# A spectral-mixer kernel: smaller first loads, a part-major tile for the first filter piece, and a fixed order of the front on each engine

## The chip, the cores and the metric

The kernel runs on one core of one Trainium2 chip. The metric is the device time of one execution in microseconds (us); lower is better. The runs of one kernel mostly lie within one per cent of each other, and all but one count as undisturbed ("fast", granted TensorE clock 0.996 to 1.0). The one slow run belongs to one experiment (`e12_all`) and is left out of its ratio. Each profile shows one execution, so small differences between two profiles are those of single runs.

Short names used throughout: PE is the matmul engine (TensorE), DVE is VectorE, ACT is ScalarE, POOL is GpSimd, SP is SyncE. Times "at 21.48" are us from the start of the profiled span.

## The reference, cut to what matters

```
def reference(A_x, A_w_r, A_w_i, B_x, B_w1, B_b1, B_w2, B_b2):
    # A: layernorm, 2-D real FFT, product with a complex filter, inverse FFT
    X = rfft2(layernorm(x));  X = X * (w_r + 1j * w_i);  y = irfft2(X)
    h = x + y
    # B: layernorm, token-mixing MLP over the 2048 positions
    h2 = h + mlp(layernorm(h))          # 2048 -> 1376 -> 2048, gelu between
    return h2
```

x is 1 x 2048 x 512 in bf16, and the filter is 2048 x 257, real and imaginary. The kernel does the FFTs as matmuls. Its stages, and the names that the code and the profile give them:

1. **Front.** Load X in pieces and the DFT factors FP in four pieces. Layernorm statistics of 16 slices (`bn`/`ag` on DVE, or two ACT passes `s1`/`s2`), their reciprocal root `rs` on ACT, then the factors scaled by it (`fs`: FS<-FP,rs). Matmuls `f1`, evicted to Y.
2. **V stage.** Eight units u = 0 to 7. For each: matmuls `f2`, evicted to CS; matmuls `x`; the product with the filter on DVE (`v`: V<-ps,W); matmuls `g1`, evicted to PQ.
3. `g2`, `g3` and the additions on DVE (TT, H, HH).
4. The MLP on PE alone, the output additions (OUT) and the stores.

## The kernel before: the parts that matter

The order of the instructions on each engine is not written by hand. Each operation is declared with its inputs, its outputs, an assumed duration and a priority. A list scheduler in the kernel then picks, step by step, the ready operation with the earliest start, and takes the higher priority on a tie:

```
    def schedule(self):
        ...
        while len(order) < len(ops):
            best = None
            for o in ready:
                ...                       # PSUM bank free? limit of open units reached?
                st = max(eng_free[o.stream], o.dep_ready, avail, o.not_before)
                key = (st, -o.prio, o.idx)
                if best is None or key < best[0]:
                    best = (key, o, st, bank)
            ...
            eng_free[e] = st + o.occ
            if o.is_dma:
                x0 = max(st + (3200.0 if st < 4000.0 else 1700.0), dma_free)
                dma_free = x0 + o.bytes / o.rate
```

The scheduled order is then final: the engine runs it as listed.

The loads of the front and of the first filter piece (12 issues: for real and imaginary part w, two components, three kinds of rows):

```
    for q, (a, b) in enumerate(((0, 2), (2, 4), (4, 6), (6, 8), (8, 12))):
        ldx(a, b, 90 - q)                 # on SyncE; ldx(0, 2) is 256 KB
    ...
    ldf(0, 90, "act")                     # FP pieces of 256 KB; these two on ScalarE
    ...
    ldf(1, 87, "act", 1800.0)
    ...
        for w, dram in ((0, A_w_r), (1, A_w_i)):
            for comp in range(2):
                d = W[comp::4, g0:g0 + ng, w, :]
                lst.append(dma(f"ld_wp{ch}_{w}{comp}", d, ...))
                d = W[2 + comp::4, h0:h0 + nh, w, :]
                lst.append(dma(f"ld_wm{ch}_{w}{comp}", d, ...))
                if g0 == 0:
                    d = W[2 + comp::4, 0, w, :]
                    lst.append(dma(f"ld_wz{ch}_{w}{comp}", d, ...))
```

The V stage of one unit. The `x` matmuls need both CS tiles of the unit, and the multiply needs all eight `x` matmuls:

```
    def stage_x(u):
        unit = PsumUnit("x", 2)
        grp = [cs_ops[2 * u + 1]]
        for i in range(2):
            G = 2 * u + i
            ...
                    mm(f"x_{G}_{c}{r}", ..., CS[rows, G, :, c, :], unit, ..., 13, 256, half=True, after=grp)
        ...
        nh = 2 if u in V_SPLIT else 1     # V_SPLIT = (0, 7): two halves by group
        for h in range(nh):
            ...
            K.op(f"v_{u}_{h}", "dve", tt, ins=[wt], outs=[vout], occ=50.0 + 2130.0 / nh, ...)
```

## Time and profile before

| | before |
|---|---|
| device time, median of 3 (range) | 134.13 us (133.91 to 134.17) |
| profiled execution, and its span | 133.9 us, 132.4 us |
| first X pieces landed | 4.87 us |
| first `f2` matmul | 18.62 us |
| V multiplies on DVE | 21.48 to 39.36 us, without a gap |
| first TT addition | 42.63 us |
| last OUT addition ends, to the end of the device time | 3.92 us |

Almost half of the span (68 to 129 us) is bound by PE alone, at full clock, and apart from the loads the change works on the first 68 us only. The busy shares show this. Each digit is the busy share of one fortieth of the span (3.3 us) in tenths:

```profile
PE   6989989999977979999999999999999999999990
DVE  0499867999981999999960000000242332423322
ACT  4579976978966999986689322222000000000000
PEclk9999999999999999999999999999999999999999
```

The chain of work that ended last, in order of time (start, duration, what ran), has these long pieces in the first 43 us:

```profile
0.72 4.15 DMA X<-in_A_x_dram
4.89 1.34 ACT JK L549 x4
6.51 0.95 POOL FS L633
...
17.10 1.47 ACT Y L549 x3
18.62 2.77 PE ps L531 x25
21.48 1.04 DVE V L739
22.62 15.62 DVE V L739 x8
38.38 0.62 PE ps L531 x8
...
42.63 0.42 DVE TT L790
```

Read it as a relay: the first load until 4.87, then statistics and POOL and ACT in turn until 18.6, a short stretch of PE, and then DVE's multiplies end to end. DVE's own list of that stretch gives start, duration, operation and count, and in brackets the idle time just before and what ended it:

```profile
19.86 0.69 DVE L712 CAST CS<-ps 128x512 bf16<-128x512 f32 x1 [0.92 <-PE ps L531]
21.48 17.88 DVE L739 TENSOR_TENSOR V<-ps,W 128x1024 bf16<-128x1024 f32 x10 [0.94 <-PE ps L531]
42.63 0.42 DVE L790 TENSOR_TENSOR TT<-ps,X 128x256 f32<-128x256 f32 x1 [3.27 <-PE ps L531]
```

Ten multiplies, 17.88 us, one line: no idle time between them. In the front, DVE's list shows what waits for the loads:

```profile
4.89 0.70 DVE L653 BATCH_NORM_STATS2 st<-X 128x6 f32<-128x512 bf16 x1 [3.78 <-DMA X<-in_A_x_dram]
...
6.13 1.35 DVE L653 BATCH_NORM_STATS2 st<-X 128x6 f32<-128x512 bf16 x2 [0.32 <-DMA X<-in_A_x_dram]
```

And the windows view (length, then busy time and count of PE, weight loads, DVE, ACT, POOL, then granted clock, DMA share and GB/s) shows ACT full between 10 us and the first `f2`, busy for 8.53 of 8.60 us:

```profile
10.00:18.60 8.60, 8.05 (x62) 5.49 (x62) 7.61 (x24) 8.53 (x23) 7.02 (x13) 1.00 0.89 260
```

### The profile page before, as it was taken

What the parts mean: (1) busy time and instruction counts of PE and PEld (TensorE: products, weight loads), DVE (VectorE), ACT (ScalarE), POOL (GpSimd) and SP (SyncE); (2) the same over time, 40 slices, a digit from 0 to 9 for tenths busy, and PEclk for the clock granted to TensorE, in tenths of its full rate; (3) what the DMA queues carried; (4) which work ended last, traced back from release to release, by engine and by line L of the source; (5) the groups of instructions that cost most, each with busy time, mean ns of one, the idle gap of its engine ahead of it and who ended that gap; (6) DMA issues with size and microseconds to landing.
All of it is one profiled execution on the core that took longest, in us unless ns stands there. A gap on an engine that the chain in (4) does not pass through costs nothing.

```text
span 132.4 us, 2013 instructions
## 1 busy us (share of the span) xinstructions
PE 123.7 (93%) x776; PEld 74.5 (56%) x786; DVE 69.3 (52%) x127; ACT 63.3 (48%) x146; POOL 12.4 (9%) x33
## 2 busy tenths in 40 slices
PE   6989989999977979999999999999999999999990
PEld 2436656788666736544434444456666666666660
DVE  0499867999981999999960000000242332423322
ACT  4579976978966999986689322222000000000000
POOL 0199920000300000000000000000000000000000
PEclk9999999999999999999999999999999999999999
DMA  2999699999999999992000000000111112111121
GB/s 80 375 396 364 153 244 273 286 322 283 419 426 417 410 408 411 417 295 74 0 0 0 0 0 0 5 0 0 40 40 70 49 40 82 42 57 62 40 79 40
DMA packets 16648, 22.16 MB, mean 167 GB/s; under 512 B 2720, under 2 KB 12960, under 8 KB 16128
## 3 DMA queue, kind: packets, MB, share of 16 engines
q1 hardware_dynamic: 16352, 21.52, 47.5%
q10 hardware_dynamic: 288, 0.52, 1.1%
q8 instruction: 6, 0.10, 0.3%
q14 instruction: 2, 0.02, 0.0%
HBM read 19.95 MB, written 2.10 MB: 167 GB/s over the span
## 4 chain that ended last, share of the span: by engine, by line
PE 51%; DVE 32%; ACT 9%; DMA 3%; POOL 2%; issue 1%; DVEq 0%; ACTq 0%
PE ps L531 50%; DVE V L739 13%; DVE H L799 7%; ACT Y L549 5%; DVE TT L790 4%; DVE TT L792 4%; DVE HH L804 4%; DMA X<-in_A_x_dram 3%; POOL FS L633 1%; ACT rs L549 1%; ACT FS L549 1%; ACT JK L549 1%; DVE OUT L829 1%; ACT PQ L549 0%; PE ps L621 0%
## 5 line engine op out<-in xcount | busy, mean ns | idle before, releaser
L531 PE MATMUL ps<-HH,W 128*128 128x512 bf16 (+1 forms) x173 | 40.3, 379 | 1.3 <-DVE HH L804 0.9
L531 PE MATMUL ps<-GT,W 128*128 128x512 bf16 (+1 forms) x172 | 37.9, 379 | 0.2
L829 DVE SCALAR_TENSOR_TENSOR OUT<-ps,B2f,H 128x512 bf16<-128x512 f32 x16 | 12.0, 750 | 48.7 <-PE ps L531 48.7
L531 PEld LDWEIGHTS ps<-GT,W 128*128 128x128 bf16 (+1 forms) x176 | 25.3, 144 | 12.8
L531 PEld LDWEIGHTS ps<-HH,W 128*128 128x128 bf16 (+1 forms) x176 | 17.2, 100 | 21.2 <-DVE HH L804 1.9
L739 DVE TENSOR_TENSOR V<-ps,W 128x2048 bf16<-128x2048 f32 (+1 forms) x10 | 17.9, 1856 | 0.9 <-PE ps L531 0.9
L549 ACT ACTIVATE GT<-ps,B1f 128x512 bf16<-128x512 f32 (+1 forms) x11 | 7.1, 689 | 14.6 <-PE ps L531 14.6
L549 ACT ACTIVATE JK<-H,nm 128x512 bf16<-128x512 bf16 x16 | 11.6, 722 | 3.0 <-DVE H L799 2.9
L653 DVE BATCH_NORM_STATS2 st<-X 128x6 f32<-128x512 bf16 x14 | 9.2, 669 | 4.1 <-DMA X<-in_A_x_dram 4.1
L621 PE MATMUL ps<-ZT 128*128 128x512 bf16 x32 | 9.6, 434 | 1.6 <-DVE ZT L617 1.2
L799 DVE TENSOR_TENSOR H<-ps,TT 128x512 bf16<-128x512 f32 x16 | 10.9, 682 | 0.0
L549 ACT ACTIVATE PQ<-ps 128x512 bf16<-128x512 f32 x16 | 8.9, 602 | 3.5 <-PE ps L531 3.3
L531 PE MATMUL ps<-EM,PQ 128*128 128x256 bf16 x64 | 9.0, 273 | 0.8 <-ACT PQ L549 0.7
L531 PE MATMUL ps<-EM,V 128*128 128x128 bf16 x128 | 9.2, 219 | 0.5 <-DVE V L739 0.5
L549 ACT ACTIVATE EO<-ps 128x512 bf16<-128x512 f32 x16 | 9.2, 596 | 0.9 <-PE ps L531 0.9
L549 ACT ACTIVATE CS<-ps 128x512 bf16<-128x512 f32 x15 | 8.3, 607 | 2.1 <-PE ps L531 2.1
L531 PE MATMUL ps<-EM,Y 128*128 128x256 bf16 x64 | 8.7, 273 | 0.4 <-ACT Y L549 0.4
L531 PE MATMUL ps<-FS,X 128*128 128x256 bf16 x64 | 8.4, 274 | 0.5 <-POOL FS L633 0.4
L531 PEld LDWEIGHTS ps<-EM,V 128*128 128x128 bf16 x128 | 7.5, 98 | 2.3 <-issue 1.4
L633 POOL TENSOR_SCALAR FS<-FP,rs 128x256 bf16<-128x256 bf16 x9 | 8.6, 965 | 0.6 <-ACT rs L549 0.5
L790 DVE TENSOR_TENSOR TT<-ps,X 128x256 f32<-128x256 f32 x16 | 6.7, 417 | 3.3 <-PE ps L531 3.3
L531 PEld LDWEIGHTS ps<-EM,PQ 128*128 128x128 bf16 x64 | 6.2, 98 | 2.9 <-ACT PQ L549 0.9
(36 smaller groups left out, 79.1 us busy)
## 6 DMA issues: line engine op xcount, KB each, us to landing
W<-in_B_w_dram SPq DMA_DIRECT2D x4, 1376.0 KB, 11.7
W<-in_B_w_dram SPq DMA_DIRECT2D x10, 512.0 KB, 18.3
out_dram<-OUT SPq DMA_DIRECT2D x16, 128.0 KB, 1.7
W<-in_A_w_r_dram SPq DMA_DIRECT2D x4, 257.0 KB, 4.5
W<-in_A_w_i_dram SPq DMA_DIRECT2D x4, 257.0 KB, 5.0
X<-in_A_x_dram SPq DMA_DIRECT2D x4, 256.0 KB, 5.0
X<-in_A_x_dram SPq DMA_DIRECT2D x2, 512.0 KB, 6.6
W<-in_A_w_r_dram SPq DMA_DIRECT2D x4, 192.8 KB, 3.3
```

What stands on the lines that cost most here:

```text
L531: return K.op(name, "pe", lambda eng, bank: eng.matmul(outf(bank), lhsT, rhs, start=start, stop=stop), ins=ins or [lhsT, rhs], occ=occ, la ...
L549: return eng.activation(dst, s, func, **kw)
L621: return K.op(name, "pe", lambda eng, bank: eng.matmul(ps[:, bank, :], ZT[:, 0:NP], ZT[:, :], start=True, stop=True), ins=[ZT[:, :]], occ= ...
L633: dve(f"fs{i}", lambda eng, bank: eng.tensor_scalar(FS[:, i, :, :], FP[:, i, :, :], rs, None, op0=ALU.mult), [FP[:, i, :, :], rs], [FS[:, ...
L653: dve(f"st_{i}", lambda eng, bank, i=i, x=x: eng.bn_stats(ST[:, i, 0:6], x), [x], [ST[:, i, 0:6]], 512, prio=25)
L739: return eng.tensor_tensor(vout, s, win, ALU.mult)
L790: dve(f"tl_{s2}", lambda eng, bank, tt=tt, xl=xl: eng.tensor_tensor(tt[:, 0, :], ps[:, bank, 256:512], xl, ALU.add), [xl], [tt[:, 0, :]], ...
L792: dve(f"th_{s2}", lambda eng, bank, tt=tt, xh=xh: eng.tensor_tensor(tt[:, 1, :], xh, ps[:, bank, 256:512], ALU.subtract), [xh], [tt[:, 1, ...
L799: return eng.tensor_tensor(hs.rearrange("p (h d) -> p h d", h=2), e, tt[:, :, :], ALU.add)
L804: dve(f"hh_{s2}", lambda eng, bank, s2=s2, hs=hs: eng.tensor_scalar(HH[:, s2, :], hs, NM[:, s2:s2 + 1], R2[:, s2:s2 + 1], op0=ALU.add, op1 ...
L829: dve(f"fin{s2}", lambda eng, bank, dst=dst, bia=bia, hs=hs: eng.scalar_tensor_tensor(dst, ps[:, bank, :], bia, hs, op0=ALU.add, op1=ALU.add),
```

## The change

Its intent: start the statistics earlier (a first X piece of 128 KB, with the two FP pieces held behind a short zero fill), balance the front over the engines in an order that is listed in the kernel and so fixed, and load the first filter piece with 8 issues instead of 12 into a tile W0 of its own, in which real and imaginary part are the outer index. The two first multiplies then split by part instead of by group. The core of the diff:

```diff
 def _row(sign, comp, k2, s):
-    return 4 * (k2 * 2 + s) + 2 * sign + comp
+    return 4 * (k2 * 2 + s) + 2 * comp + sign
...
+                if o.name in pos and done[pos[o.name][0]] != pos[o.name][1]:
+                    continue             # fixed order for the named operations of an engine
...
-                x0 = max(st + (3200.0 if st < 4000.0 else 1700.0), dma_free)
-                dma_free = x0 + o.bytes / o.rate
+                x0 = max(st + 1750.0, dma_free) + o.stall
+                dma_free = x0 + o.bytes / (min(o.rate, 340.0) if x0 < 7000.0 else o.rate)
...
-STAT_ACT = (1, 3)
...
+STAT_ACT = (3, 6)
+FS_ENG = {4: 'act', 7: 'act', 9: 'act', 12: 'dve', 14: 'dve'}
...
+FRONT = {
+    "dve": """bn_0 bn_1 ag_1 ag_0 bn_2 bn_4 bn_5 ag_2 bn_7 ...""",
+    "act": """rs_1 rs_0 s1_3 s2_3 rs_3 s1_6 rs_2 s2_6 rs_4 ...""",
+    "pool": """fs_1 fs_0 bv_3 fs_3 fs_2 bv_6 fs_5 fs_6 ...""",
+    "pe": """f1_1 f1_0 f1_3 f1_4 f1_5 f1_2 f1_6 ...""",
+}
-V_SPLIT = (0, 7)
+V_SPLIT = (7,)
...
-    for q, (a, b) in enumerate(((0, 2), (2, 4), (4, 6), (6, 8), (8, 12))):
-        ldx(a, b, 90 - q)
+    for q, (a, b) in enumerate(((0, 1), (1, 2), (2, 4), (4, 6), (6, 8), (8, 12))):
+        ldx(a, b, 99 - q)
...
-    ldf(0, 90, "act")
-    ldf(1, 87, "act", 1800.0)
+    ldf(0, 92, "act", after=[zt])
+    ldf(1, 91, "act", after=[zt])
-    dma("ld_E", ...)
-    dma("ld_MR", ...)
+    dma("ld_EMR", ...)
...
+            if g0 == 0:
+                d = W0[0:NP:2, w, :, :].rearrange("p g l -> p (g l)")
+                lst.append(dma(f"ld_wp{ch}_{w}", d, ...))
+                d = W0[1:NP:2, w, 0, :]
+                lst.append(dma(f"ld_wz{ch}_{w}", d, ...))
...
+        if u == 0:
+            for w in range(2):
+                wt = W0[:, w, :, :]
...
+                K.op(f"v_0_{w}", "dve", tw, ins=[wt], outs=[vout], occ=1115.0, lat=1235.0, ...)
+            return
```

Also: the Y evictions become partly 1024 columns wide, two small POOL operations per ACT-computed statistic become one ahead of its `rs`, and the limit of open `f1` units rises from 6 to 7. For the V stage of units 1 to 7 the diff changes only the row order of the filter and of the matrices that go with it (`_row`), not the operations.

## The prediction

> **What bounds the kernel now.** The page gives 132.4 us of span, PE busy 93%, DVE 52%. The chain that ended last splits it into stretches with different limits:
> - 0.7 to 4.9 us: the first X piece is loading (DMA, 4.15 us).
> - 4.9 to 18.6 us: statistics, scaled DFT factors FS, Y evictions. First ACT and GpSimd in turn (FS on POOL, 0.95 us each), from about 10 us ACT: the windows show it busy 8.53 of 8.60 us.
> - 18.6 to 21.5: F2 and X matmuls (2.8 us), then VectorE: ten V multiplies without a gap (21.5 to 39.4), and from 42.6 to 68 the TT/H/HH operations (DVE busy 25.33 of 25.4 us).
> - 68 to 129: PE alone, clock 1.0.
>
> Everything after 18.6 us is saturated on DVE or PE, and the change leaves its work as it was. So only the front can gain.
>
> **What the change does.**
> 1. The first load becomes 128 KB alone on SyncE; ScalarE issues its two FP pieces only after the 0.27 us zero fill. Before, X0 (256 KB) and FP0 (256 KB) start together at 0.72 us and share the engines: DMA moves nothing until about 2.3 us and runs at 390 GB/s from 3.0, and X0 lands at 4.87. My estimate: x0 at about 3.4, x1 about 4.0, FP0 about 4.6 us. The Trainium skill (DMA: Bandwidth & Descriptors, "Issuing engines are not separate DMA queues") says that issuing from several engines saves only issue time, so total landing (x4 on) should not move.
> 2. First FS on POOL starts at about 5.4 instead of 6.51 us. But 20 warm-up matmuls hold PE until about 7.1, and the FS chain on POOL becomes longer: 11 scalings (0.93 us pitch) and two small ones against 9.
> 3. ScalarE in the front: same four statistics passes, 12 rs against 13, same three FS, evictions of 6144 instead of 6656 columns in 10 instead of 13 instructions. At 0.49 us per 512 columns, with about 0.06 us fixed per instruction, that is about 0.6 us less. VectorE takes 512 columns more, two FS fewer.
> 4. First filter piece: 8 issues instead of 12. At 0.65 us each, later loads are issued about 2.6 us earlier. Off the critical path: DVE never waited for W.
> 5. The first two V multiplies split by real/imaginary part, not by group: same 2 x 1.2 us.
>
> Adding the measured durations along each engine's new order (the same sum for the old order gives F2 at 18.5 against 18.62 measured), the three engines become nearly level: last POOL FS ends near 16.7, last Y evictions near 17.7 us, F2 starts at about 17.8, the first V multiply at 20.5 instead of 21.48. With landings 0.5 us later it is 18.2 and 20.9; earlier ones give nothing more.
>
> **Prediction.** A gain of about 0.9 us (0.3 to 1.6), which the saturated rest passes on unchanged: 133.2 us, 132.5 to 133.9. Chances: faster by over 2% 0.04, within 2% 0.94, slower 0.02.
>
> **What would show it.** x0 landing before 3.8 us; first bn_stats at 3.4 instead of 4.89; first POOL FS about 5.4; F2 near 17.8; V's length unchanged at 17.9 us, only shifted; 42.6-to-68 and the PE stretch shifted, not shortened.
>
> **What would make it wrong.** x0 not landing early (start-up latency rather than sharing); POOL stalling on bv_3 or FP pieces; 1024-column evictions slower per column than 512; the new order on PE in the V stage or its tail (38.2 to 42.6 us) opening or closing a gap.

## The result, and the profile after

| | before | after | predicted |
|---|---|---|---|
| device time, median of 4 (range) | 134.12 us (133.91 to 134.17) | 134.79 us (134.68 to 134.96) | 133.2 (132.5 to 133.9) |
| profiled execution | 133.9 us | 134.96 us | |
| first statistics start | 4.89 | 3.18 | 3.4 |
| first FS on POOL | 6.51 | 6.06 | 5.4 |
| first `f2` matmul | 18.62 | 18.54 | 17.8 |
| first V multiply | 21.48 | 21.24 | 20.5 |
| last V multiply ends | 39.36 | 40.22 | 38.4 (20.5 + 17.9) |
| end of V to first TT | 3.27 | 3.27 | shifted only |
| last OUT to the end of the device time | 3.92 | 4.12 | not considered |

The change made the kernel 0.5% slower: ratio 1.0054, with a 95% interval of 1.0037 to 1.0071. A ratio here is the mean time of one kernel's fast runs over the mean of the other's fast runs of the same rounds, so it is not quite the ratio of the medians quoted. That is inside 2%, but 0.67 us in the wrong direction by the medians, and outside my range.

DVE's list of the V stage after the change has what the one line of before did not have:

```profile
21.24 2.36 DVE L794 TENSOR_TENSOR V<-ps,W 128x1024 bf16<-128x1024 f32 x2 [0.94 <-PE ps L551]
23.51 8.87 DVE L807 TENSOR_TENSOR V<-ps,W 128x2048 bf16<-128x2048 f32 x4
33.47 6.75 DVE L807 TENSOR_TENSOR V<-ps,W 128x2048 bf16<-128x2048 f32 x4 [1.08 <-PE ps L551]
43.49 0.42 DVE L858 TENSOR_TENSOR TT<-ps,X 128x256 f32<-128x256 f32 x1 [3.27 <-PE ps L551]
```

Before the third line stands `[1.08 <-PE ps L551]`: DVE was idle for 1.08 us before the multiply of unit 5, and a matmul ended the wait. The chain says what PE was doing:

```profile
3.05 6.37 DMA X<-in_A_x_dram
9.45 1.29 DVE st L678 x2
...
16.59 1.82 DVE Y L736 x3
18.54 4.09 PE ps L551 x40
22.66 0.61 ACT CS L569
23.31 2.31 PE ps L551 x27
25.65 0.60 ACT PQ L569
26.30 7.15 PE ps L551 x92
33.47 5.63 DVE V L807 x3
```

From 26.30 to 33.45 PE runs 92 matmuls in one stretch without a wait, and DVE's multiplies, which were the chain from 21.48 on before, come back into it only at 33.47. The windows view of this stretch shows PE busy for all of its 7.20 us and DVE for 6.12:

```profile
26.30:33.50 7.20, 7.20 (x95) 6.13 (x96) 6.12 (x4) 6.37 (x13) 1.63 (x10) 1.00 1.02 305
```

Everything behind it is shifted, not changed: from the first TT to the end of the last OUT addition both profiles take 87.35 us. For the two profiled executions the sum closes: the V stage is 1.10 us longer (18.98 against 17.88), the front is 0.24 us shorter (21.24 against 21.48), the end is 0.20 us longer (4.12 against 3.92). Together that is +1.06, and the two executions differ by 134.96 - 133.9 = 1.06. The medians differ by only 0.67 because the profiled execution was the fastest of before and the slowest of after.

In the front, DVE's list shows the first small piece early, and the next ones not:

```profile
3.18 0.69 DVE L678 BATCH_NORM_STATS2 st<-X 128x6 f32<-128x512 bf16 x1 [2.07 <-DMA X<-in_A_x_dram]
4.72 0.69 DVE L678 BATCH_NORM_STATS2 st<-X 128x6 f32<-128x512 bf16 x1 [0.85 <-DMA X<-in_A_x_dram]
...
6.47 1.88 DVE L678 BATCH_NORM_STATS2 st<-X 128x6 f32<-128x512 bf16 x3 [0.78 <-DMA X<-in_A_x_dram]
...
9.45 1.29 DVE L678 BATCH_NORM_STATS2 st<-X 128x6 f32<-128x512 bf16 x2 [0.22 <-DMA X<-in_A_x_dram]
```

The first slice is there 1.7 us earlier than before (3.18 against 4.89), the second about 0.2 us earlier (4.72), and the third 0.34 us later (6.47 against 6.13).

### The profile page after: what moved, and what is told of

Read it like the earlier page. It is cut to its first block, busy times and chain, and to the rows that moved or that the text cites. A ratio compares the mean times of both kernels' runs of the same rounds, so it can differ in the third digit from the quotient of the medians.

```text
span 133.0 us, 2008 instructions
## 1 busy us (share of the span) xinstructions
PE 124.5 (94%) x776; PEld 75.7 (57%) x786; DVE 69.4 (52%) x126; ACT 62.6 (47%) x142; POOL 13.6 (10%) x34
## 4 chain that ended last, share of the span: by engine, by line
PE 58%; DVE 30%; DMA 5%; ACT 2%; SPq 2%; issue 1%
PE ps L551 58%; DVE H L867 7%; DMA X<-in_A_x_dram 5%; DVE V L807 4%; DVE TT L858 4%; DVE TT L860 4%; DVE HH L872 4%; DVE st L678 3%; DVE Y L736 2%; SPq L541 2%; ACT PQ L569 1%; DVE OUT L897 1%; ACT CS L569 0%; DVE FS L656 0%; ACT Y L569 0%
## 5 line engine op out<-in xcount | busy, mean ns | idle before, releaser
L551 PE MATMUL ps<-HH,W 128*128 128x512 bf16 (+1 forms) x173 | 40.4, 379 | 1.3 <-DVE HH L872 0.9
L551 PE MATMUL ps<-GT,W 128*128 128x512 bf16 (+1 forms) x172 | 37.9, 379 | 0.2
L551 PEld LDWEIGHTS ps<-GT,W 128*128 128x128 bf16 (+1 forms) x176 | 25.5, 145 | 12.6
L551 PEld LDWEIGHTS ps<-HH,W 128*128 128x128 bf16 (+1 forms) x176 | 17.2, 100 | 21.2 <-DVE HH L872 1.9
L807 DVE TENSOR_TENSOR V<-ps,W 128x2048 bf16<-128x2048 f32 (+1 forms) x8 | 15.6, 2015 | 1.1 <-PE ps L551 1.1
L644 PE MATMUL ps<-ZT 128*128 128x512 bf16 x32 | 10.6, 479 | 1.5 <-DVE ZT L589 1.2
L656 POOL TENSOR_SCALAR FS<-FP,rs 128x256 bf16<-128x256 bf16 x11 | 10.1, 933 | 5.9 <-ACT rs L569 5.9
L551 PE MATMUL ps<-EM,V 128*128 128x128 bf16 x128 | 9.5, 219 | 1.0 <-DVE V L807 1.0
L551 PE MATMUL ps<-EM,PQ 128*128 128x256 bf16 x64 | 9.0, 273 | 0.8 <-ACT PQ L569 0.7
L551 PEld LDWEIGHTS ps<-EM,V 128*128 128x128 bf16 x128 | 7.6, 98 | 3.2 <-issue 1.6
L551 PE MATMUL ps<-EM,Y 128*128 128x256 bf16 x64 | 8.6, 273 | 0.8 <-DVE Y L736 0.4
L551 PE MATMUL ps<-FS,X 128*128 128x256 bf16 x64 | 8.1, 273 | 0.0
L551 PEld LDWEIGHTS ps<-EM,PQ 128*128 128x128 bf16 x64 | 6.2, 98 | 2.9 <-ACT PQ L569 0.9
```

The costliest lines, as they stand in the source:

```text
L551: return K.op(name, "pe", lambda eng, bank: eng.matmul(outf(bank), lhsT, rhs, start=start, stop=stop), ins=ins or [lhsT, rhs], occ=occ, la ...
L644: return K.op(name, "pe", lambda eng, bank: eng.matmul(ps[:, bank, :], ZT[:, 0:NP], ZT[:, :], start=True, stop=True), ins=[ZT[:, :]], occ= ...
L656: dve(f"fs_{i}", lambda eng, bank: eng.tensor_scalar(FS[:, i, :, :], FP[:, i, :, :], rs, None, op0=ALU.mult), [FP[:, i, :, :], rs], [FS[:, ...
L807: return eng.tensor_tensor(vout, s, win, ALU.mult)
```

## The experiments

Three questions came out of the comparison: what makes the hole in the V stage, why the front gained 0.24 instead of 0.98 us, and where the extra 0.2 us at the end come from. All fifteen kernels gave correct results. Each batch ran on one chip beside runs of the kernel before, whose medians were 134.10 to 134.15 in all four batches. All times below are for fast runs, with six runs of each kernel and eleven of before.

### First batch: halves of the change

**`e1_front_only`**: the change without its filter part.

```diff
-V_SPLIT = (7,)
+V_SPLIT = (0, 7)
...
-                d = W0[0:NP:2, w, :, :].rearrange("p g l -> p (g l)")     # and the rest of the 8 issues
+                d = W[2 * comp::4, g0:g0 + ng, w, :]                       # the 12 issues of before
...
-        if u == 0:                                                        # first multiply by part
```

> The changed kernel with the old filter load (12 issues into the shared tile) and the first V multiply halved by group again; its front, issue order and evictions stay. Theory A (the 1.1 us hole before the sixth V multiply comes from the order in which PE's program places the X matmuls, which needs both parts of the change together): no VectorE hole in the V stage, V from about 21.2 to 39.1 us (17.9 us long), time about 133.9 us. Rival B (the earlier or reordered front alone makes the hole): a hole of about 1 us stays, time about 134.8.

Measured: 134.13 us (133.8 to 134.83), ratio 1.001 (0.9979 to 1.0041). The V stage has no hole: ten multiplies in 17.80 us from 21.59. So the new front alone doesn't make the hole. It also gains nothing: in its profile the third statistic started only at 7.41, `f2` at 18.90. The end takes 3.92 us, as before.

**`e2_filter_only`**: before, with the filter tile, the 8 issues and the split by part, and nothing else.

```diff
+    add("W0", [NP, 2, 4, LW], bf, region(2 * 4 * LW * 2))
...
-V_SPLIT = (0, 7)
+V_SPLIT = (7,)
...            # filter loads and first multiply as in the change; row order of the change
```

> The kernel of before with only the new first filter tile (8 issues) and the first V multiply halved by real/imaginary part. Theory A: no hole, V as long as before (17.9 us), time 134.1 us. Rival C (halving by part delays the first G1 matmuls by 1.1 us, PE falls behind, and that alone is the hole): a hole of about 1 us in the V stage and about 135.2 us.

Measured: 134.15 us (134.06 to 134.37), ratio 1.0006 (0.9982 to 1.0031). No hole either: 2.35 us for the two halves, then 15.54 us for eight multiplies. The end takes 4.05 us. Each half of the change costs next to nothing, and only both together have the hole. So neither half alone brings it. What the two halves do together is give the scheduler another starting position. Listed by name, the matmuls on PE around `x_10` and `x_11`, which feed the multiply of unit 5, stand like this ("x4" is four in a row):

```
before  ... g1_11x4 f2_11x4 f2_12x4 f2_13x3 g1_12x4 x_10x4 x_11x4 g1_13x4 g1_14x4 ...
e1      ... g1_11x4 f2_12x1 f2_13x4 x_10x4 x_11x4 g1_12x4 g1_13x4 ...
e2      ... g1_11x4 f2_12x4 x_10x4 x_11x4 g1_12x4 g1_13x4 ...
after   ... f2_11x4 f2_12x2 g1_12x4 g1_13x4 g1_14x4 g1_15x4 f2_12x2 f2_13x4 f2_14x4 x_10x4 x_11x4 ...
```

In the kernel after, 26 matmuls for other units stand between the first two `f2_12` and `x_10`. What sets it apart is the longer stretch from the `x` matmuls of unit 3 to those of unit 5, in which DVE has two multiplies of about 2.2 us to run: after has 84 matmuls other than `x` there, before 47, e1 44 and e2 43. (The number behind `f2_11` alone, 28 in after and 11 in before, does not separate the kernels: e1 has 32 and e2 28, without a hole.) In the traces the end of unit 3's `x` matmuls and the end of unit 5's are 7.95 us apart in after (25.45 and 33.40), and 4.51, 4.39 and 4.29 us in before, e1 and e2. The Trainium skill (PSUM — Partial Sum Buffer, section "Engine vs sequencer instructions") says that matmuls start and complete in program order; the trace of after agrees: its 256 `f2`, `x` and `g1` matmuls start in the program's order of these three kinds.

**`e3_v_order`**: the file that ran was an earlier draft, not the kernel that the expectation was written for. It is the kernel after with only the eight matmuls `x_10` and `x_11` moved ahead of those 26:

```diff
+V_ORDER = """... f2_12_00 f2_12_01 x_10_00 ... x_11_11 g1_12_00 ... g1_15_11 f2_12_10 f2_12_11 f2_13_00 ..."""
...
-    K.forced["pe"] = [... f1 of the front ...]
+    K.forced["pe"] = [... f1 of the front ...] + V_ORDER.split()
```

> The changed kernel with nothing altered but the order of PE's F2, X and G1 matmuls in the V stage, which is pinned to the order of e2_filter_only (same matmuls, same V multiplies). Theory A: the hole before the sixth multiply shrinks from 1.08 to under 0.3 us, V stage about 18 us, time about 133.9. Rival D (PE has too much work before the sixth multiply whatever the order; the wait only moves): V stage stays near 19.0 us and the time near 134.8.

Measured: 135.04 us (134.91 to 135.32), ratio 1.0071 (1.0047 to 1.0096): not better than after. DVE's list of this run shows what happened to the wait:

```profile
23.45 11.24 DVE L828 TENSOR_TENSOR V<-ps,W 128x2048 bf16<-128x2048 f32 x5
35.72 4.55 DVE L828 TENSOR_TENSOR V<-ps,W 128x2048 bf16<-128x2048 f32 x3 [1.03 <-PE ps L572]
```

Five multiplies now run without a gap instead of four, and the wait, 1.03 us, stands before the next. Moving one group ahead hands the debt on: PE still has the same work to do before the multiply after it (from the `x` of unit 3 to those of unit 6 it runs 95 matmuls other than `x`, in after and here; 82 in before, 75 in e2). As a test of the text above it, the run is void; as a test of "just move the late matmuls up", it is a clear no.

**`e4_fp_on_sync`**: after, with the two first FP pieces issued by SyncE behind x1 and x2, so that nothing of ScalarE's queue can share the engines with the first X pieces.

```diff
+    ldx(0, 1, 99)
+    ldx(1, 2, 98)
+    ldf(0, 97)
+    ldx(2, 4, 96)
+    ldf(1, 95)
...
-    ldf(0, 92, "act", after=[zt])
-    ldf(1, 91, "act", after=[zt])
```

> The changed kernel with both FP pieces issued on SyncE behind x1 and x2, so that x1 shares the engines with nothing. Theory E (x1 came at 4.7 instead of 4.0 us because it shares with the FP pieces of ScalarE): x1 lands at about 3.7, second statistics instruction starts at 3.8 instead of 4.72, first POOL scaling at 5.2 instead of 6.06; but VectorE still waits for the 512 KB X piece until about 9.4, so F2 starts near 18.3 instead of 18.54 and the time falls by at most 0.3 us (hole kept). Rival F (start-up of the loads is slow whatever shares them): x1 stays at 4.5 or later, nothing moves. Rival G (ScalarE's chain alone sets F2): F2 at about 17.7, time 134.0.

Measured: 135.76 us (135.08 to 136.58), ratio 1.0114 (1.0083 to 1.0145): with e8 the slowest kernel. The execution that was profiled is the slowest of the six, 136.58 us. DVE's list of it:

```profile
3.02 1.29 DVE L681 BATCH_NORM_STATS2 st<-X 128x6 f32<-128x512 bf16 x2 [1.91 <-DMA X<-in_A_x_dram]
...
6.54 0.69 DVE L681 BATCH_NORM_STATS2 st<-X 128x6 f32<-128x512 bf16 x1 [1.96 <-DMA X<-in_A_x_dram]
8.97 1.29 DVE L681 BATCH_NORM_STATS2 st<-X 128x6 f32<-128x512 bf16 x2 [1.73 <-DMA X<-in_A_x_dram]
```

Half of the idea was right: without FP beside them, x0 and x1 are both there for statistics back to back from 3.02, where after had the second at 4.72, and POOL's first scaling starts at 4.95 instead of 6.06. So it is the sharing with FP that holds x1 back. The Trainium skill (DMA: Bandwidth & Descriptors, section "Queues, rings and completion order") says that each DMA engine takes turns between the queues that have work for it, packet by packet. This pair of runs agrees as far as it goes: from 2 to 5 us, with both queues at work in after, SyncE's moved 0.37 MB and ScalarE's 0.47 MB; the turns themselves are not seen. But everything behind is late, and the rate fell. The windows of 5 to 8 us, for this kernel

```profile
5.00:8.00 3.00, 3.00 (x12) 1.20 (x11) 0.69 (x1) 1.46 (x6) 2.12 (x3) 1.00 0.84 191
```

and for after

```profile
5.00:8.00 3.00, 3.00 (x12) 1.26 (x11) 2.19 (x6) 1.82 (x6) 1.94 (x3) 1.00 1.03 354
```

give 191 GB/s against 354 in the last column. Up to 9 us this kernel had moved 1.72 MB, after 2.26, before 2.43. Issuing was not what held it up: SyncE issued x2 at 2.09 and x4 at 3.04, yet their statistics started only at 6.54 and 8.97. Nor was it that one queue cannot move more: in after ScalarE's queue was done at 5.93 us, its packets make up only about 5% of the bytes of this window, and from 6 to 8 us SyncE's alone moved 357 GB/s; and the single queue of e4 moved 409 GB/s from 9 to 13 us. Why it moved so little before that is not settled: the order of the pieces changed too, and only this one slow execution was profiled. The hole was unchanged (1.08 us), which fits: PE's order was unchanged too.

### Second batch: the order on PE, both ways

**`e5_v_order_e2`**: after, with the order of the `f2`, `x` and `g1` matmuls on PE pinned to that of `e2_filter_only`; nothing else.

```diff
+V_ORDER = """... f2_12_11 x_10_00 ... x_11_11 g1_12_00 ..."""      # the 256 matmuls in e2's order
...
-    K.forced["pe"] = [... f1 of the front ...]
+    K.forced["pe"] = [... f1 of the front ...] + V_ORDER.split()
```

> What e3_v_order was announced as: the changed kernel with the order of all F2, X and G1 matmuls on PE pinned to that of e2_filter_only. (The file that ran as e3_v_order was an older one, in which only the eight X matmuls of the sixth multiply were moved ahead of 26 others; its hole of 1.03 us moved on to the seventh multiply.) Theory A (order): V stage 17.9 to 18.2 us without a hole over 0.3 us, time 133.7 to 133.9. Rival D (PE has too much work, the wait only moves, as it did in e3_v_order): V stage 19.0 us, time 134.8 to 135.0.

Measured: 134.15 us (133.9 to 134.43), ratio 1.0007 (0.9982 to 1.0033).

```profile
21.14 2.36 DVE L815 TENSOR_TENSOR V<-ps,W 128x1024 bf16<-128x1024 f32 x2 [0.93 <-PE ps L572]
23.41 13.33 DVE L828 TENSOR_TENSOR V<-ps,W 128x2048 bf16<-128x2048 f32 x6
36.94 2.36 DVE L828 TENSOR_TENSOR V<-ps,W 128x1024 bf16<-128x1024 f32 x2 [0.20 <-PE ps L572]
42.57 0.42 DVE L879 TENSOR_TENSOR TT<-ps,X 128x256 f32<-128x256 f32 x1 [3.27 <-PE ps L572]
```

The wait falls from 1.08 to 0.20 us, and the first TT comes at 42.57 instead of 43.49. The slowdown against before is gone, but there is no gain either.

**`e8_hole_in_before`**: the reverse. Before, with after's order of the same matmuls.

```diff
+V_ORDER = """... f2_12_01 g1_12_00 ... f2_14_11 x_10_00 ..."""     # the 256 matmuls in after's order
+    K.forced["pe"] = V_ORDER.split()
```

> The kernel of before, with nothing altered but the order of PE's F2, X and G1 matmuls, which is pinned to the changed kernel's. Theory A: holes of 1 us or more in the V stage that before does not have, time 135.2 to 135.8. Rival C/D (the hole needs the multiply halved by part, or the earlier start): no hole, time 134.1.

Measured: 135.62 us (135.34 to 136.14), ratio 1.0116 (1.0089 to 1.0143), with holes of 0.53 and 1.09 us in a kernel whose loads, front and operations are all those of before:

```profile
21.24 8.95 DVE L768 TENSOR_TENSOR V<-ps,W 128x1024 bf16<-128x1024 f32 x5 [0.93 <-PE ps L560]
30.72 2.29 DVE L768 TENSOR_TENSOR V<-ps,W 128x2048 bf16<-128x2048 f32 x1 [0.53 <-PE ps L560]
34.10 6.75 DVE L768 TENSOR_TENSOR V<-ps,W 128x2048 bf16<-128x2048 f32 x4 [1.09 <-PE ps L560]
```

Taking the order away removes the hole; putting it in makes it. With this pair the cause is shown.

**`e6_old_loads`**: e5 with before's front loads (x0 and x1 as one piece of 256 KB, FP on ScalarE without the wait for the zero fill).

```diff
-    for q, (a, b) in enumerate(((0, 1), (1, 2), (2, 4), (4, 6), (6, 8), (8, 12))):
+    for q, (a, b) in enumerate(((0, 2), (2, 4), (4, 6), (6, 8), (8, 12))):
...
-    ldf(0, 92, "act", after=[zt])
-    ldf(1, 91, "act", after=[zt])
+    ldf(0, 97, "act")
+    ldf(1, 91, "act")
```

> As e5_v_order_e2, with the loads of the front as before (first X piece 256 KB, FP0 at once on ScalarE). Theory H (the new front's gain rests on the early first pieces; its fewer evictions do not help because the first scaling would come at 6.7 and rs_3 at 9.0): F2 at about 19.1, time 134.4, slower than e5 by 0.5. Rival I (what the new front gains is the lighter ScalarE chain, not the loads): F2 at 18.4 or earlier, time at or below e5.

Measured: 134.63 us (134.53 to 135.04), ratio 1.0047 (1.0019 to 1.0074). Statistics from 4.63, `f2` at 18.91, V at 21.61, against 18.44 and 21.14 in e5. So the new loads are worth about 0.47 us at the first multiply in these two profiles once the front's order is the new one; the medians, 0.48 us apart, agree, and the six runs of each do not overlap.

**`e7_first_256`**: e5 with x0 and x1 as one piece of 256 KB, FP still behind the zero fill.

```diff
-    for q, (a, b) in enumerate(((0, 1), (1, 2), (2, 4), (4, 6), (6, 8), (8, 12))):
+    for q, (a, b) in enumerate(((0, 2), (2, 4), (4, 6), (6, 8), (8, 12))):
```

> As e5_v_order_e2, with x0 and x1 in one 256 KB piece again, ahead of the FP pieces as in the change. Theory J (1 KB rows of the two 128 KB pieces and their extra issue delay what follows): both land by 4.1, x2 by 5.9, the 512 KB piece by 9.0 instead of 9.42; F2 18.2, time 0.2 to 0.4 us below e5. Rival E (x1 is late only by sharing with FP): the pair lands at 4.6 or later, x2 unchanged, time as e5.

Measured: 134.27 us (134.03 to 134.59), ratio 1.0014 (0.9989 to 1.004). Statistics from 4.18 for both slices, the third at 6.11 (e5: 6.67), `f2` at 18.46, V at 21.16: level with e5. Theory J's landings came, but not its gain, and rival E's late landing did not come. So the part of the load change that helped is holding FP back, not splitting the first piece.

### Third batch: the end, and the short chain in the front

Over all runs the time from the end of the last OUT addition to the end of the device time goes with the number of DMA copies that SyncE issues: 3.92 or 3.93 us with 74 (before, e1, e8), 3.95 with 72 (e4), 4.05 to 4.16 with 70 (after, e2, e3, e5), 4.21 and 4.24 with 69 (e6, e7). The work in this stretch is the same. Theory K was that the count does it.

**`e9_sp_pad`**: e5 with four small loads more on SyncE in the middle of the MLP (which makes 74 again), and their semaphore in the final waits.

```diff
+    for n in range(4):
+        dma(f"ld_pad{n}", T["PAD"][:, n, :], B_b2.rearrange(...), 4096, ..., not_before=80000.0, group="pad")
...
-    K.emit(es, ["dq_st"] + [...])
+    K.emit(es, ["dq_st"] + [...] + ["dq_pad"])
```

> As e5_v_order_e2, with four more 4 KB loads on SyncE at about 60 us, into a tile that nobody reads; the number of loads and stores on SyncE and ScalarE is then 74 as before (70 in the changed kernel). From the end of the last output addition to the end of the measured time it took 3.92 us in before, e1 and e8 (74), 3.95 in e4 (72), 4.05 to 4.16 in after, e2, e3, e5 (70), 4.21 to 4.24 in e6, e7 (69). Theory K (the length of SyncE's program sets when its last instructions are fetched): 3.9 us again, time 0.2 below e5, about 133.95. Rival L (it is the new filter tile or its loads themselves): 4.1 to 4.2 stays, time as e5.

Measured: 134.69 us (134.2 to 134.75), ratio 1.0024 (0.9998 to 1.005), end 4.30 us: slower than either theory had it. I took this for the end of theory K, but it does not show that. The run has a final wait more, so two things changed at once. From the last OUT addition to the span's end it took 2.50 us (e5: 2.15; before, also with 74 copies: 2.38), and from there to the end of the device time 1.79 us (e5: 2.01; before: 1.54). Theory K stays open here; e14 below leaves the added wait out.

**`e10_bv_first`**: e5 with POOL's small operation `bv_3` ahead of its second scaling, so that `rs_3` on ACT waits less.

```diff
-    "pool": """fs_1 fs_0 bv_3 fs_3 ...""",
+    "pool": """fs_1 bv_3 fs_0 fs_3 ...""",
```

> As e5_v_order_e2, with bv_3 ahead of the second scaling on POOL. Theory M (the gapless run of ScalarE starts at rs_3, which waits for bv_3 behind two POOL scalings): rs_3 at about 7.6 instead of 8.3 and ScalarE's run 0.5 to 0.7 earlier until rs_9, where it meets VectorE's statistics (ag_9 at 13.9); F2 0 to 0.3 us earlier, time 133.9 to 134.15. Rival G (ScalarE alone sets F2): F2 0.6 us earlier, time 133.5.

Measured: 134.22 us (133.61 to 134.74), ratio 0.9988 (0.9955 to 1.0022). The profiled execution had the third statistic only at 7.59, so its `rs_3` came at 8.96 and V at 22.08: the spread of the loads was larger than what was to be seen. Inconclusive.

**`e11_bv_ag_fs`**: e10, with `ag_9` right behind `ag_8`, one scaling moved from POOL to DVE, and the `x_14`/`x_15` matmuls five places earlier (the text below says ten; the edit moves them past five `g1`).

```diff
-... ag_8 bn_12 ag_9 bn_13 ... fs_12 ys_7 fs_14 ...
+... ag_8 ag_9 bn_12 bn_13 ... fs_12 fs_13 ys_7 fs_14 ...
-... g1_22_11 g1_23_00 x_14_00 ...
+... x_14_00 ... x_15_11 g1_22_00 ...
```

> As e10_bv_first, and ag_9 directly after bn_9, the scaling of piece 13 on VectorE instead of POOL, and the X matmuls of the last multiply ahead of ten G1 matmuls. Theory N (three engines bind the front together: each alone gives little, all relieved give the rest): F2 at 17.8 to 18.0, no hole over 0.1 us in the V stage, time 133.4 to 133.6. Rival (loads of X decide by 14 us): F2 stays at 18.3 or later, time 133.9 or more.

Measured: 133.97 us (133.53 to 134.68), ratio 0.998 (0.9946 to 1.0014). `f2` at 18.38, V from 21.08, no hole, first TT at 42.17. Theory N's `f2` at 17.8 to 18.0 was missed; its rival's reading, 18.3 or later, came. The hole is not shown to be closed by the earlier `x_14`: e13 and e15 have the same order and 0.21 and 0.20 us of wait before the last two halves, and e10, whose V started late, has none without it.

**`e12_all`**: e11 with the four small loads and the wait of e9 (the diffs of e11 and e9 together).

> e11_bv_ag_fs with the four padding loads of e9_sp_pad: if K and N hold, 133.2 to 133.4 us, faster than both kernels; under L as e11.

Measured: 134.86 us (134.38 to 135.74) in the five fast runs; the slow one took 136.4. Ratio 1.0047 (1.001 to 1.0084); the third statistic at 7.16, end 4.30 us as in e9. Nothing gained.

### Fourth batch: the end again, and the best version

By now another number stood out. Some small DMA transfers are instruction fetches (the page lists them as queues q8 and q14, kind "instruction"), and the last 8 KB one starts after the last instruction of the span:

| kernels | DMA copies on SyncE | last 8 KB fetch, us after the span's end | us from last OUT to the end |
|---|---|---|---|
| e9, e12 (with one wait more) | 74 | 0.30, 0.31 | 4.30, 4.30 |
| before, e1, e8 | 74 | 0.60 to 0.61 | 3.92 to 3.93 |
| e14 | 73 | 1.03 | 3.93 |
| e4, e15 | 72 | 1.11, 1.08 | 3.95, 3.93 |
| after, e2, e3, e5, e10, e11 | 70 | 1.68 to 1.69 | 4.02 to 4.16 |
| e6, e7, e13 | 69 | 1.86 to 1.87 | 4.21 to 4.34 |

Theory K2, which the first three batches suggested and the fourth tested, is that what counts is where this fetch falls: about 1 us behind the span's end it costs nothing, later it does. The two kernels with one final wait more (e9, e12) are outside it: their fetch is the earliest, and their end is long. What the added wait costs there was not measured alone. Apart from these two, the number of copies and the place of the fetch go together in every row, so these runs can't tell theory K2 from theory K.

**`e13_256_e11`**: e11 with the first piece of 256 KB, as in e7.

```diff
-    for q, (a, b) in enumerate(((0, 1), (1, 2), (2, 4), (4, 6), (6, 8), (8, 12))):
+    for q, (a, b) in enumerate(((0, 2), (2, 4), (4, 6), (6, 8), (8, 12))):
```

> e11_bv_ag_fs with x0 and x1 in one 256 KB piece, as in e7_first_256. In the runs whose first X piece has 256 KB (before, e2, e6, e7, e8) x2 was there at 6.06 to 6.17 us; in those with two 128 KB pieces (after, e1, e3, e5, e9 to e12) at 6.47 to 7.59, and their times scatter. Theory O (two small first pieces push x2 and what follows back, and this ate the front's gain): x2 at 6.1, rs_3 at 7.5, F2 at 18.0 to 18.2, time 133.4 to 133.7 with a range under 0.6 us. Rival (VectorE's and POOL's chains bind anyway): F2 18.4 as in e7 and e11, time 134.0.

Measured: 133.84 us (133.53 to 134.09), ratio 0.9979 (0.9955 to 1.0003). Third statistic at 5.96, `f2` at 18.14 as theory O had it, V at 20.84: the earliest of all profiles, 0.34 us behind what I had predicted for the change itself. The end is the longest, 4.34 us.

**`e14_pad3`**: e5 with three small loads more on SyncE, and no added wait (the first hunk of e9 with `range(3)`).

> e5_v_order_e2 with three small loads more on SyncE at about 60 us and no wait for them (73 loads and stores on SyncE). In e9_sp_pad the last instruction fetch moved from 1.7 us after the span to 0.3, but the final barrier inside the span grew by 0.35 us; with 72 and 74 (e4, before) it came 1.1 and 0.6 us after the span and the end was shortest. Theory K2 (where that fetch falls decides the end): fetch about 0.85 us after the span, 3.9 us from the last output addition to the end of the measured time, time 0.2 below e5, 133.95. Rival L (the new filter tile or its loads lengthen the end): 4.1 or more, time as e5.

Measured: 133.87 us (133.69 to 134.11), ratio 0.9981 (0.9956 to 1.0007). The end is 3.93 us, against 4.16 in e5, and V starts at 21.23: three loads that do nothing took about 0.2 us off the end. The medians of the two kernels are 0.28 us apart, from two batches, and their intervals overlap. K2 holds here, and so does K; rival L, that the filter tile or its loads lengthen the end, falls.

**`e15_best`**: e13 with the three small loads of e14.

> e13_256_e11 with the three loads of e14_pad3. If O and K2 hold, 133.2 to 133.5 us, faster than both kernels; if only one, about 133.6.

Measured: 133.95 us (133.29 to 134.28), ratio 0.998 (0.9952 to 1.0007). The end is 3.93 us, as K2 (and K) has it; but `f2` came at 18.47 and V at 21.17, later than in e13, so the two gains did not add up in this run.

The four best, e11 and e13 to e15, are about 0.2% faster than before and about 0.7% faster than after (whose ratio to before, 1.0054, comes from another batch). Their intervals still include 1, so a version that certainly beats before was not found.

## Why the prediction was wrong, point by point

1. **The step that failed** is "Everything after 18.6 us is saturated on DVE or PE, and the change leaves its work as it was. So only the front can gain", and with it "a gain [...] which the saturated rest passes on unchanged" and "V's length unchanged at 17.9 us". The work was unchanged; its order on PE was not. The V stage took 18.98 us, with 1.08 us of wait before unit 5. That DVE is saturated in a stage says that nothing can be gained there by feeding it sooner, not that nothing can be lost: PE fed it with little to spare (busy for 17.03 of the 18.00 us from 21.4 to 39.4 in before), and one re-ordering was enough. e5 and e8 show the cause from both sides. My list of doubts did name "the new order on PE in the V stage"; I did not look at it, though the kernel's order can be read without a run. Even the scheduler's own plan had the gap: the multiply of unit 4 planned to end at 30.72 and that of unit 5 to begin at 31.55, while before's plan had none. Those planned times rest on assumed durations and are no measurement, but the gap in them was a reason to look. The other kernels' own plans have their holes too, where the chip had them: 0.14 us in e5 (0.20 measured), 1.00 in e3 (1.03), 0.49 and 1.16 in e8 (0.53 and 1.09), and none in e1 and e2. The scheduler picks one operation at a time and compares no whole plans; the planned end of the V stage was the same as before's within 0.05 us. Which of its inputs tips the order is not settled; e1 and e2 show that it takes both halves of the change.

2. **The front gained 0.24 us instead of 0.98.** That the front starts earlier was right, and the terms that were mis-sized are landings. I put x1 at 4.0 and POOL's first scaling at 5.4; x1 was used at 4.72 and the scaling came at 6.06, 0.66 us late. `f2` came at 18.54, 0.74 us later than predicted. That the one passed into the other is not shown: in after's own profile the wait that ended last in the front is that for the 512 KB piece x8, issued at 3.05 and landed at 9.42; from 9.45 to `f2` DVE and ACT follow each other without a pause over 0.14 us. In e5, whose front is the same, the chain goes through x1, POOL's first two scalings and ACT instead. So the paths are nearly level, and which of the late landings counts changes from run to run. My own note, "with landings 0.5 us later it is 18.2 and 20.9", goes the right way. I had counted on the first pieces going ahead of FP; in e4, with no FP beside them, both slices were there at 3.02, so the sharing is what held x1 itself back. The three engines did become nearly level: between 10.0 and 18.5 us ACT was busy 8.48, DVE 7.89 and POOL 7.91 of 8.50 us.

3. **"Total landing (x4 on) should not move"** was wrong in part. I took it from the Trainium skill (DMA: Bandwidth & Descriptors, "Issuing engines are not separate DMA queues"). But that section speaks of which engine issues, and the change leaves that as it was (both first FP pieces stay on ScalarE); the step from there to the landings was mine. After had moved 2.26 MB by 9 us against 2.43 before, and its 512 KB piece x8 was still being waited for at 9.45. With everything on one queue (e4) it was 1.72 MB. In the runs whose first piece was 256 KB (before, e2, e6, e7, e8, e13, e15) the third statistic started at 5.96 to 6.17; with two pieces of 128 KB on the same two queues it was 6.47 to 7.59. The pairs e5 and e7, e11 and e13 differ in nothing but the split (6.67 against 6.11, 6.59 against 5.96), so splitting the first piece goes with the later third statistic. One part of it is plain: SyncE issues x2 one issue later, at 1.63 instead of 1.17. Whether that is all of it stays open.

4. **The end got 0.20 us longer.** I had not considered that fewer issues on SyncE could cost anything. The number of copies and the place of the last fetch both fit all runs but the two with an added final wait, and adding three idle loads gives the time back (e14, e15). Which of the two counts, and how, is not shown.

5. **What held:** x0 before 3.8 us (3.18), the statistics in place of 4.89 at about 3.4 (3.18), the two halves of the first V multiply at the same cost (2.36 us for both), and the stretches behind the V stage shifted only (3.27 us from V to TT in both). The doubt about wide evictions did not come true: in the chain of e5 ACT takes 0.91 us for 1024 columns and 0.48 for 512.

With the hole removed (e5) the change stands at before's time: its profile has 0.34 us won up to the first V multiply (21.14 against 21.48), and a V stage 0.28 us longer (18.16 against 17.88, with the wait of 0.20 in it) and a 0.24 us longer end (4.16 against 3.92) take that back.

## What to carry to other kernels

When a scheduler in the kernel decides the order, a change to one stage is a change to all later ones: before predicting, compare the order of the feeding engine in the stage that bounds the kernel, and count how much work stands between one group that the busy engine waits for and the next ones. Where the scheduler plans times, look for gaps in its plan. A late group is not mended by moving that group alone (e3): the order that feeds a saturated engine has to be right over the whole stage, so pin it when it is good. And in this kernel the second small piece was early only with nothing else in flight beside it, while moving the FP pieces in between on the same queue cost more than the sharing did (e4).

## What the Trainium skill lacked or had wrong

- DMA: Bandwidth & Descriptors, "Issuing engines are not separate DMA queues": it says that issuing from several engines saves only the sequencer's issue time, "usually small relative to the DMA itself". The runs do not contradict it. The same early loads in another order from SyncE alone moved 191 GB/s between 5 and 8 us instead of 354, and the kernel was 1 us slower (135.76 against 134.79), but in after about 95% of this window came from SyncE's queue as well. What kept the early loads of e4 so slow, no page and no run here says.
- The same page, "Queues, rings and completion order": the turns between queues are stated, but not what they do to a small first load. Beside two 256 KB pieces on another queue, the second 128 KB piece was used at 4.72 us; alone, both were used from 3.02 us on.
- Runtime: NRT & Kernel Launch, "Instruction fetch mechanics": it has the fetch in 16 KiB blocks and mostly hidden. The trace shows 16 KB fetches on one queue and 8 KB ones on another, and one of 8 KB that starts 0.3 to 1.9 us after the last instruction. Among kernels with the same final waits, the later it comes, the longer the end: 3.92 us at 0.6, up to 4.34 us at 1.86. No page has this; that the fetch is the cause is not shown.
